# A table-driven cross-attention and maxout kernel: W's first three slices in nine pieces, and a new order for the head

## The chip, the core and the metric

The kernel runs on one core of a Trainium2 chip. The core has a matrix engine (PE, with its weight loads shown as PEld), a vector engine (DVE), a scalar engine (ACT), GpSimd (POOL) and a sync engine (SP) that here only issues transfers. The engines run side by side, each through its own list of instructions in order, and wait for each other through semaphores. Transfers of all queues run on the same 16 DMA engines. The metric is the time of one execution in microseconds (us), the median of three runs. It was 152.32 us before the change (152.24 to 152.41).

## What is computed

There are 8 batches of x with 8 heads, 512 tokens and 64 channels, and a state of 32 rows for each head. Two attentions run between them, and the result goes through a maxout layer with three weight matrices and an output layer:

```python
scores = scale * np.matmul(x, state.transpose(0, 1, 3, 2))   # a: softmax over the 32 states
xread = np.matmul(a, state)
scores2 = scale * np.matmul(state, x.transpose(0, 1, 3, 2))  # a2: softmax over the 512 tokens
sread = np.matmul(a2, x)
...
h = np.maximum(np.maximum(x @ w1, x @ w2), x @ w3)
return (h @ w_out).astype(np.float32)
```

In the last two lines `x` stands for the concatenated xread and sread, 544 tokens of each batch with 512 channels. w1, w2 and w3 are 512 by 768, w_out is 768 by 512.

## The kernel before

The kernel does not form xread. For each batch it multiplies the state into W first, which gives G = state x (w1, w2, w3), 256 rows by 3 x 768 columns. Then one matmul of the attention weights with G gives the first layer before the maximum. The 768 columns are cut into six slices of 128, numbered 0 to 5. "Slice m" of W is columns 128m to 128m+127 of all three matrices. A slice of G for a batch needs that slice of W from all three matrices.

What happens is written in tables of short operations (`FIRST`, `EACH`, `LAST`), and `perform` calls a function for each in turn. The text order sets, engine by engine, the order in which instructions stand; the order between engines comes from semaphores alone. `FIRST` holds the head: loading, batches 0 and 1, and the beginning of batch 2. `EACH` is one steady batch, and `LAST` the end. The operations that matter here, with the batch as first number:

- `lw m0 m1 i` (line 179) loads columns of slices m0 to m1-1 of matrix i, cast from float32 to bf16, on POOL's queue. A piece of one slice is 128 KB in bf16, with rows of 256 bytes; a piece of two slices is 256 KB, with rows of 512 bytes.
- `lxg b g`, `lx b` (lines 168, 163) load half or all of a batch of x on POOL's queue. `lst k` (line 152) loads the state of batches 2k and 2k+1, 128 KB of float32, on the queue of the engine named. `lwo` loads w_out.
- `xt`, `xtc` turn x on PE and copy it out of PSUM; `xtd` turns it by a DMA transpose from SP. `sc`, `ex`, `sum`, `wt` are scores, exponentials (ACT), sums (DVE) and attention weights; `at`, `atc` or `atd` turn these; `sr`, `srs` are sread.
- `g b m` (line 363) makes slice m of G for batch b, eight small matmuls, and `gc` copies it out of PSUM. `gr`, `grc` do the same for a run of columns. A `gc` or `grc` with `A` goes on ACT, with `D` on DVE, with `AD` half and half.
- `l1 b m` (line 416) is slice m of the first layer: six matmuls of 512 columns into three PSUM banks. `m0` (ACT), `ma`, `mb` (DVE) are its evictions, and free one bank each.
- `l2 b j`, `l2c` are the output layer for a quarter of the tokens and its copy; `so` stores.
- `stc`, `stt`, `stp` cast, turn and place a pair of states. `pad` (POOL) makes the padded copy of x for `sr`. `busy n` runs n matmuls of zeros that nothing reads.

PSUM is handed out by two strings: `BANKS` names one of four single banks for each use in turn, `PAIRS` one of two double banks. G's slices and a batch's scores take a pair, everything else a bank. A use waits for the copy that empties the bank.

A transfer on POOL's queue counts on one of eight semaphores in turn, so the ninth waits until the first has landed.

## Time and profile before

| | |
|---|---|
| runs | 152.32 us median of 3 (152.24 to 152.41) |
| profiled execution, span from first to last instruction | 151.4 us |
| median of the runs less that span | 0.9 us |
| granted TensorE clock | 1.000 of full speed |
| DVE, ACT, POOL busy | 118.9, 82.8, 57.0 us |
| moved by DMA | 22.29 MB, mean 147 GB/s |

The profile is of one execution. Times in it count from the span's start. In the lists of issues the last number is the time from the start of a transfer's issue to its landing; where a row holds several issues it is their median. Bytes of a transfer are counted as they are written, so a W piece of 128 KB was read as 256 KB.

### The profile page before, as it was taken

What the parts mean: (1) busy time and instruction counts of PE and PEld (TensorE: products, weight loads), DVE (VectorE), ACT (ScalarE), POOL (GpSimd) and SP (SyncE); (2) the same over time, 40 slices, a digit from 0 to 9 for tenths busy, and PEclk for the clock granted to TensorE, in tenths of its full rate; (3) what the DMA queues carried; (4) which work ended last, traced back from release to release, by engine and by line L of the source; (5) the groups of instructions that cost most, each with busy time, mean ns of one, the idle gap of its engine ahead of it and who ended that gap; (6) DMA issues with size and microseconds to landing.
All of it is one profiled execution on the core that took longest, in us unless ns stands there. A gap on an engine that the chain in (4) does not pass through costs nothing.

```text
span 151.4 us, 3635 instructions
## 1 busy us (share of the span) xinstructions
PE 146.4 (97%) x1431; PEld 73.8 (49%) x1431; DVE 118.9 (79%) x204; ACT 82.8 (55%) x143; POOL 57.0 (38%) x79
## 2 busy tenths in 40 slices
PE   6999799999999999999999999999999999999992
PEld 2566343335445443544354435443544446679771
DVE  6477698999977898879987988798879887675353
ACT  3368558976364665466646664666466653331220
POOL 6979650561528505540554046414331200001500
PEclk9999999999999999999999999999999999999999
DMA  3999999979737979999589749974503250300455
GB/s 115 211 189 195 207 198 195 151 149 139 139 74 167 230 59 265 129 223 132 155 124 230 144 130 140 232 122 141 218 0 78 68 226 4 122 18 17 175 180 196
DMA packets 39108, 22.29 MB, mean 147 GB/s; under 512 B 23072, under 2 KB 36896, under 8 KB 39088
## 3 DMA queue, kind: packets, MB, share of 16 engines
q0 software_dynamic: 15872, 13.96, 48.7%
q1 hardware_dynamic: 21776, 6.82, 23.4%
q10 hardware_dynamic: 1440, 1.25, 2.7%
q8 instruction: 12, 0.20, 0.5%
q14 instruction: 8, 0.07, 0.2%
HBM read 15.20 MB, written 8.91 MB: 159 GB/s over the span
## 4 chain that ended last, share of the span: by engine, by line
PE 86%; DMA 6%; POOL 4%; issue 1%; DVE 1%; POOLq 0%
PE pw L416 46%; PE po L447 25%; DMA w<-in_moe_w_dram 6%; PE pg L363 5%; PE po L462 4%; POOL w L179 2%; PE ps L262 2%; PE psr L327 2%; POOL x L168 1%; PE pgh L363 1%; PE pt L222 1%; DVE held L522 0%; PE idle L520 0%; PE idle L211 0%; DVE osb L466 0%
## 5 line engine op out<-in xcount | busy, mean ns | idle before, releaser
L416 PE MATMUL pw<-aT,G 128*128 128x512 bf16 x288 | 66.8, 379 | 0.0
L431 ACT CAST t<-pw 128x512 bf16<-128x512 f32 (+1 forms) x54 | 30.4, 564 | 28.9 <-PE pw L416 27.2
L416 PEld LDWEIGHTS <-G 128*128 128x128 bf16 x288 | 27.2, 98 | 33.2 <-issue 1.9
L436 DVE TENSOR_TENSOR t<-t,pw 128x512 bf16<-128x512 bf16 (+1 forms) x54 | 35.4, 655 | 9.5 <-ACT t L431 7.4
L447 PE MATMUL po<-wout,ht 128*128 128x512 bf16 x168 | 39.9, 379 | 0.0
L440 DVE TENSOR_TENSOR ht<-t,pw 128x512 bf16<-128x512 bf16 x48 | 32.9, 687 | 4.3
L447 PEld LDWEIGHTS <-ht 128*128 128x128 bf16 x168 | 15.3, 98 | 19.0 <-issue 1.7
L284 POOL TENSOR_TENSOR a<-e,rden 128x1024 bf16<-128x1024 bf16 (+1 forms) x9 | 14.5, 1620 | 24.1 <-ACT osb L454 11.1
L477 POOL DMA_DIRECT2D out_dram<-osb x13 | 7.4, 572 | 30.5 <-ACT t L431 27.5
L403 ACT CAST G<-pg 128x1024 bf16<-128x1024 f32 (+1 forms) x17 | 14.3, 875 | 1.3 <-PE pg L363 1.3
L311 POOL COPY xp<-x 128x1024 bf16<-128x1024 bf16 x12 | 12.3, 1062 | 5.5 <-DMA x<-in_x_dram 5.5
L454 DVE COPY osb<-po 128x512 f32<-128x512 f32 x16 | 10.9, 684 | 2.4 <-PE po L447 2.3
L276 DVE TENSOR_REDUCE seen<-e 128x32 f32<-128x1024 bf16 (+1 forms) x10 | 10.0, 999 | 3.6 <-ACT e L269 3.6
L403 DVE CAST G<-pg 128x1024 bf16<-128x1024 f32 (+1 forms) x13 | 12.2, 972 | 0.7 <-ACT G L403 0.7
L454 ACT COPY osb<-po 128x512 f32<-128x512 f32 x13 | 7.7, 593 | 8.9 <-PE po L447 8.9
L269 ACT ACTIVATE e<-ps 128x1024 bf16<-128x1024 f32 (+1 forms) x10 | 8.5, 854 | 6.6 <-PE ps L262 6.4
L363 PE MATMUL pg<-w,bd 64*32 64x512 bf16 (+1 forms) x288 | 10.8, 362 | 0.9 <-DMA w<-in_moe_w_dram 0.9
L211 PE MATMUL idle<-zero 128*128 128x512 bf16 x27 | 10.0, 477 | 1.3 <-DVE zero L187 1.3
L472 POOL DMA_DIRECT2D out_dram<-osb x4 | 2.2, 544 | 19.4 <-ACT osb L466 19.4
L381 ACT CAST G<-pg 128x768 bf16<-128x768 f32 x9 | 7.1, 801 | 3.3 <-PE pg L363 3.1
L416 PE MATMUL pw<-atp,w 128*128 128x256 bf16 x72 | 8.7, 272 | 0.0
L416 PEld LDWEIGHTS <-w 128*128 128x128 bf16 x72 | 6.9, 98 | 1.5
(70 smaller groups left out, 116.0 us busy)
## 6 DMA issues: line engine op xcount, KB each, us to landing
out_dram<-osb POOLq DMA_DIRECT2D x12, 512.0 KB, 3.5
x<-in_x_dram POOLq DMA_DIRECT2D x4, 512.0 KB, 7.3
x<-in_x_dram POOLq DMA_DIRECT2D x7, 256.0 KB, 5.5
w<-in_moe_w_dram POOLq DMA_DIRECT2D x4, 256.0 KB, 7.5
w<-in_moe_w_dram POOLq DMA_DIRECT2D x2, 384.0 KB, 7.9
wout<-in_moe_w_out_dram POOLq DMA_DIRECT2D x1, 768.0 KB, 11.6
out_dram<-osb SPq DMA_DIRECT2D x3, 256.0 KB, 2.4
osb<-in_x_dram SPq DMA_DIRECT2D x1, 512.0 KB, 4.0
```

Source lines behind the costliest of these rows:

```text
L211: nc.tensor.matmul(p, zero[:, 0:128], zero, start=True, stop=True)
L276: nc.vector.reduce_sum(out=den, in_=parity(e[b], g), axis=AX.X)
L284: times[c](out=parity(a[b], g).rearrange("p j g s n -> p j (g s) n"), in0=parity(e[b], g).rearrange("p j g s n -> p j (g s) n"), in1=rdens ...
L311: nc.gpsimd.tensor_copy(out=xp[b][:, :, :, g * (D + 1):g * (D + 1) + D], in_=v[:, g])
L363: nc.tensor.matmul(p(s, g), bd(b, 2 * s + g)[64 * g:64 * g + 64, g, :], f(w_sb[64 * g:64 * g + 64, s]), start=True, stop=True, tile_positi ...
L403: copier[c[g]](out=v[:, g:h], in_=p[:, g:h, 0:c1 - c0])
L416: nc.tensor.matmul(pw[i][:, 0:n], lhs(i, k), rhs(k), start=(k == 0), stop=(k == nk - 1))
L431: nc.scalar.copy(out=t0s[b, m][:, 0:n], in_=open_ps["l", b, m][0][:, 0:n])
L436: nc.vector.tensor_max(t1s[b, m][:, 0:n], t0s.pop((b, m))[:, 0:n], open_ps["l", b, m][1][:, 0:n])
L440: nc.vector.tensor_max(ht[b][:, m, :], t1s.pop((b, m))[:, 0:n], open_ps.pop(("l", b, m))[2][:, 0:n])
L447: nc.tensor.matmul(p, ht[b][:, m, j * 128:(j + 1) * 128], wout_sb[:, m, :], start=(m == 0), stop=(m == NM - 1))
L454: copier[c[i]](out=o[:, j, i * w:i * w + w], in_=p[:, i * w:i * w + w])
```

## The change

The tables `FIRST`, `EACH` and `LAST` become one table `PLAN`, written out for all batches. The code for the operations stays, with these differences: buffers of the rotating tiles are named in a table `PLACES`; the states' bf16 copies share two buffers where they had four; tiles are taken when they are first written, not when the matmuls ahead of them start; and the exponentials are written with the token quarters in the order 0, 2, 1, 3, which `sr` and the output layer then read in that order (`turned`). Operations for turning the scores by DMA (`sq`, `eq`, `etd`, `std`) are added to the list of operations, and the plan has none of them.

```diff
+    xt 1 0; ex 0 1; sum 0 0; busy 1; busy 1; xt 1 1; lw 0 1 2; xones 0; lw 0 1 1; lw 0 1 0; sum 0 1; xtc 1 1 D;
+    xtc 1 0 A; sc 1 0; lw 1 2 1; lw 1 2 2; lw 1 2 0; ex 1 0; lst 3 A; wt 0 1 D; lw 2 3 0; busy 1; busy 1;
...
-        nc.scalar.activation(out=parity(e[b], g), in_=open_ps.pop(("s", b, g)), func=AF.Exp, scale=scale)
+        new(e, b, [128, J, 2, HS, Ns], "e")
+        nc.scalar.activation(
+            out=parity(e[b], g).rearrange("p (c i) g s n -> p i c (g s n)", i=2),
+            in_=open_ps.pop(("s", b, g)).rearrange("p (i c) g s n -> p i c (g s n)", i=2),
+            func=AF.Exp, scale=scale)
...
+    def turned(j):
+        return j % 2 * 2 + j // 2
...
+    def buffer(shape, dtype, tag, key, name=None):
+        n = places[tag][str(key)] if places else str((B if key == "s" else key) % 2)
+        return work.tile(shape, dtype, tag=tag + n, bufs=1, name=name or tag)
...
-    perform(FIRST)
-    for b in range(2, B - 1):
-        perform(EACH, b)
-    perform(LAST)
+    perform(PLAN)
```

From batch 3's scores to the end the order on every engine is the one before (on PE, 1885 of some 2850 instructions of the main path). All that moves lies ahead of that: the head. 28 matmuls of zeros become 20. Three places follow.

**POOL, the loads of W.** Before, behind the last loads of batch 1's x. `x_87` is that x, `w` the weights, `a<-e,rden` the attention weights of batch 0 or 1.

```order
L168 DMA x_87<-in_x_dram 128x4x256 x2
L179 DMA w<-in_moe_w_dram 128x4x256 x2
L179 DMA w<-in_moe_w_dram 128x4x128
L179 DMA w<-in_moe_w_dram 128x4x256
L179 DMA w<-in_moe_w_dram 128x4x128 x2
L284 TENSOR_TENSOR a<-e,rden 128x4x128 x2
L198 MEMSET x_86 128x64
L179 DMA w<-in_moe_w_dram 128x4x128
L179 DMA w<-in_moe_w_dram 128x4x384 x2
L179 DMA w<-in_moe_w_dram 128x4x256
L284 TENSOR_TENSOR a<-e,rden 128x4x128
```

Now, at the same place:

```order
L206 DMA x_83<-in_x_dram 128x4x256 x2
L217 DMA w<-in_moe_w_dram 128x4x128
L236 MEMSET x_82 128x64
L217 DMA w<-in_moe_w_dram 128x4x128 x6
L349 TENSOR_TENSOR a<-e,rden 128x4x128
L217 DMA w<-in_moe_w_dram 128x4x128 x2
L217 DMA w<-in_moe_w_dram 128x4x384
L349 TENSOR_TENSOR a<-e,rden 128x4x128
L217 DMA w<-in_moe_w_dram 128x4x384
L217 DMA w<-in_moe_w_dram 128x4x128
L217 DMA w<-in_moe_w_dram 128x4x256
```

The first three slices came in six pieces, three of them of two slices; now they come in nine pieces of one slice, slice by slice. Slice 0 of all matrices stands behind three pieces of 384 KB in sum, where it stood behind three of 640 KB. Seven pieces stand ahead of the first product on POOL, where six stood; of three products on POOL one went to DVE. Of the pieces behind, those of slice 3 (two of 384 KB for slices 3 to 5 of two matrices, one of 128 KB for the third) now have the small one last.

**PE, the first layer's first slices.** Before, at the end of `l1 0 0` (`pw_427` is its third bank, `pg` a slice of G):

```order
L416 LDWEIGHTS G
L416 MATMUL pw_427<-aT,G 128x512 [waits DVE_49]
...
L363 LDWEIGHTS bd_82 [waits DMASW7_49,DMASW0_49]
L363 MATMUL pg<-w,bd_82 32x384 [waits Activation_49]
L363 LDWEIGHTS bd_82
```

Now, from the end of `l1 0 0` (`pw_424`) through `l1 0 1` (`pw_439` to `pw_441`):

```order
L477 MATMUL pw_424<-aT,G 128x512
L477 LDWEIGHTS G [waits Activation_49]
L477 MATMUL pw_439<-aT,G 128x512 [waits DVE_49]
...
L477 MATMUL pw_440<-aT,G 128x512 [waits Activation_49]
...
L477 MATMUL pw_441<-aT,G 128x512 [waits DVE_49]
...
L427 LDWEIGHTS bd_78 [waits DMASW3_49,DMASW2_49,DMASW1_49]
L427 MATMUL pg<-w,bd_78 32x384 [waits Activation_49]
```

Slice 2 of G for batches 0 and 1 stood right behind `l1 0 0`; now `l1 0 1`, six matmuls, comes ahead of it. Both turns of batch 1's weights (`at 1 0`, `at 1 1`) now come ahead of `l1 0 0`; one came behind slice 2 of G. Behind slice 2 there were four first-layer slices, now there are three, and then in both programs slice 3 of G for both batches.

**ACT, ahead of batch 2's exponentials.** Before, `e<-ps` being those exponentials, `t` an eviction `m0`, `bd` a placed state:

```order
L403 CAST G<-pg 128x2x512
L431 CAST t_691<-pw_645 128x512
L381 CAST G<-pg 128x6x128
L431 CAST t_748<-pw_680 128x512
L403 CAST G<-pg 128x512
L431 CAST t_757<-pw_715 128x512
L269 ACTIVATE e<-ps 128x1024
L228 COPY bd_84<-pt 64x16x32 x2
```

Now:

```order
L466 CAST G<-pg 128x2x512
L492 CAST t_632<-pw_621 128x512
L466 CAST G<-pg 128x2x512
L444 CAST G<-pg 128x6x128
L492 CAST t_670<-pw_655 128x512
L492 CAST t_702<-pw_692 128x512
L444 CAST G<-pg 128x6x128
L492 CAST t_726<-pw_708 128x512
L466 CAST G<-pg 128x2x512
L313 ACTIVATE e<-ps 128x2x2x256
L271 COPY bd_80<-pt 64x16x32 x2
```

Two whole copies of G that DVE did, one in full and one in half, are on ACT now, and `stp 1`, which the two shared, is on ACT alone. DVE has half of `gc 1 3` and the cast of a state in exchange.

Some more moves. `lst 3` and `lst 2` stood behind slice 3 of G (on SP and ACT) and are now issued on ACT with `lst 1`, just behind batch 1's exponentials. `stt 3` and `stt 2` stand together ahead of batch 2's scores, where one stood ahead and one behind. On POOL, `ones`, which waits for w_out, stands ahead of `pad 2`, and `lxg 3` behind it. On SP, `atd 2` stands ahead of `xtd 3`; the product `wt 2` that it turns went from POOL to DVE.

More of the change, by code (lines that the diff above doesn't have):

```diff
@@ new lines @@
+    ma 1 2; gc 0 4 A; l1 0 3; m0 0 3; stc 2 P; ones; gc 0 5 D; mb 1 2; gr 2 0 512; ma 0 3; gr 2 1792 2304;
+    l1 1 3; grc 2 0 512 A; m0 1 3; mb 0 3; grc 2 1792 2304 A; stc 3 D; ma 1 3; pad 2; g 1 4; mb 1 3; lxg 3 1;
+    l1 0 5; lxg 3 0; pad 3; gc 1 4 A; m0 0 5; ma 0 5; g 1 5; gr 2 1280 1792; l1 1 4; mb 0 5; m0 1 4; gc 1 5 A;
+    ma 1 4; mb 1 4; l1 0 4; gr 2 512 1024; m0 0 4; grc 2 1280 1792 A; ma 0 4; stt 3; stt 2; mb 0 4; sc 2 -;
+    l2 0 1; l2 0 0; ex 2 -; stp 2 A; sum 2 -; stp 3 A; l2 0 3; l2c 0 1 A; l2c 0 0 A; l1 1 5; wt 2 - D;
@@ L530 @@
-        "sc": (scores, 1), "ex": (exps, 1), "sum": (sums, 1), "wt": (weights, 1), "at": (a_turn, 1),
-        "atc": (a_turned, 1), "atd": (a_turn_dma, 1), "pad": (pad, 1), "sr": (sread, 1),
-        "srs": (sread_scale, 1), "srt": (sread_turn, 1), "ap": (sread_place, 1), "g": (g_slice, 1), "gc": (g_sliced, 1),
-        "gr": (g_run, 1), "grc": (g_ran, 1), "l1": (layer1, 1), "l1s": (layer1_states, 0),
-        "m0": (max_first, 1), "ma": (max_second, 1), "mb": (max_third, 1), "l2": (layer2, 1), "l2c": (layer2_out, 1),
@@ new lines @@
+        "stp": states_place, "std": states_turn_dma, "sts": states_place, "xt": x_turn, "xtc": x_turned, "xtd": x_turn_dma,
+        "sc": scores, "ex": exps, "sq": scores_turned, "eq": exps_turned, "etd": e_turn_dma, "sum": sums, "wt": weights, "at": a_turn,
+        "atc": a_turned, "atd": a_turn_dma, "pad": pad, "sr": sread,
+        "srs": sread_scale, "srt": sread_turn, "ap": sread_place, "g": g_slice, "gc": g_sliced,
+        "gr": g_run, "gq": lambda b, c0, c1: g_run(b, c0, c1, True), "gqc": g_ran, "grc": g_ran, "l1": layer1, "l1s": layer1_states,
```

248 lines of the change are left out of this document (148 added, 100 removed), and 3 rows, old and new, of the table BANKS.

## The prediction

> **What bounds the kernel now.** I read the page first, for the share of each engine.
>
> ```profile
> span 151.4 us, 3635 instructions
> PE 146.4 (97%) x1431; PEld 73.8 (49%) x1431; DVE 118.9 (79%) x204; ACT 82.8 (55%) x143; POOL 57.0 (38%) x79
> ```
>
> PE is busy all along, but zeros count there too, so the page cannot say when useful work becomes dense. The chain of waits can (start, length, what).
>
> ```profile
> 8.17 9.70 DMA w<-in_moe_w_dram
> ...
> 17.91 0.52 PE pg L363 x16
> ...
> 18.75 0.22 PE pat L295 x4
> 18.97 5.20 PE pw L416 x24
> 24.17 0.45 PE pg L363 x16
> 24.62 0.33 PE pt L222 x4
> 24.95 1.40 PE pw L416 x6
> ...
> 35.51 0.47 PE ps L262 x16
> ...
> 41.16 0.22 PE pt L222 x4
> ...
> 47.72 0.47 PE ps L262 x16
> ...
> 148.20 0.02 issue
> ```
>
> From 17.91 to 148.20 the chain is PE alone, and before that one load of W. So the time is the moment from which PE works without a gap, plus the work that is left. PE's own timeline shows how long it stood still there:
>
> ```profile
> 17.91 0.52 PE L363 MATMUL pg<-w,bd 64*32 64x384 bf16 x16 [0.86 <-DMA w<-in_moe_w_dram]
> ```
>
> The gap itself is 0.86 us, for slice 2 of G. Three points serve as milestones, since what lies between them can be counted in both programs: slice 3 of G (24.17), batch 2's scores (35.51) and batch 3's scores (47.72). From the last on, every engine has its old order, so I carry 47.72 to the end as it is.
>
> **When W lands.** Start and length of issues on POOL, and below them issues with the time to landing, each from a narrow window:
>
> ```profile
> 3.67 0.75 POOL L168 DMA_DIRECT2D x<-in_x_dram  x1
> 4.40 1.58 POOL L179 DMA_DIRECT2D w<-in_moe_w_dram  x2
> 5.97 1.50 POOL L179 DMA_DIRECT2D w<-in_moe_w_dram  x2
> 7.44 1.51 POOL L179 DMA_DIRECT2D w<-in_moe_w_dram  x2
> 13.66 1.50 POOL L179 DMA_DIRECT2D w<-in_moe_w_dram  x2
> ...
> x<-in_x_dram POOLq DMA_DIRECT2D x1, 256.0 KB, 6.0
> w<-in_moe_w_dram POOLq DMA_DIRECT2D x1, 256.0 KB, 6.7
> ...
> w<-in_moe_w_dram POOLq DMA_DIRECT2D x1, 256.0 KB, 7.3
> w<-in_moe_w_dram POOLq DMA_DIRECT2D x1, 128.0 KB, 7.2
> ...
> w<-in_moe_w_dram POOLq DMA_DIRECT2D x1, 256.0 KB, 7.8
> w<-in_moe_w_dram POOLq DMA_DIRECT2D x1, 128.0 KB, 7.8
> ...
> w<-in_moe_w_dram POOLq DMA_DIRECT2D x1, 384.0 KB, 8.6
> ```
>
> Added up: batch 1's x is there at 3.67 + 6.0 = 9.7. W's first pieces follow at 11.1, 12.4, 13.2 (5.97 + 7.2), 14.5 and 15.2 (7.44 + 7.8). The sixth, issued at 8.2, took the longest, 9.70, to 17.9 (the chain's first row). The last piece with slice 3 lands at 13.66 + 8.6 = 22.3. Landings follow each other in the order of issue, a queue that is always full; what counts is what stands ahead in it, not when a piece is issued.
>
> From these, a piece of two slices takes 1.33 us (11.1 to 12.4), one of one slice 0.74 (12.4 to 13.2 and 14.5 to 15.2). The change takes three pieces of two slices apart: 3 x (2 x 0.74 - 1.33) = 0.45 us more at most; half of it, if the rounding to 0.1 us of each landing goes the other way. I take 0.35. POOL issues in 0.75 a piece, as fast as pieces move, but seven are issued by 4.40 + 7 x 0.76 + 0.2 = 9.9, with x in the queue until 9.7, so it never runs dry there.
>
> The Trainium skill's "DMA: Bandwidth & Descriptors" (§ Specifications) asks for at least 512 bytes a transfer for the full rate and names a read-modify-write below; rows of one slice are 256 bytes as written. The rows above agree in sign only: 0.74 against half of 1.33.
>
> The state loads are the second cost. One was issued at 12.26, and the windows show what moved (last column GB/s):
>
> ```profile
> 12.26 0.35 ACTq L152 DMA_DIRECT2D stf<-in_state_dram  x1
> ...
> 13.00:14.00 1.00, 1.00 (x22) 0.47 (x20) 0.97 (x3) 0.89 (x2) 1.00 (x2) 1.00 1.62 186
> 14.00:15.00 1.00, 1.00 (x45) 0.72 (x44) 1.00 (x2) 0.66 (x2) 1.00 (x2) 1.00 1.72 207
> 15.00:16.00 1.00, 1.00 (x22) 0.45 (x20) 0.93 (x5) 0.95 (x3) 0.35 (x2) 1.00 1.61 228
> ```
>
> In the two us from 14 to 16, 435 KB moved where W alone makes 2 x 186 = 372. Of the 435, 131 are the state's 128 KB, so W got 304 and lost 68 KB, 0.37 us. Had a state load cost by its bytes, it would be 131/186 = 0.70. Two more loads now stand ahead of slice 3: 0.7 us by the first price, 1.4 by the second. I take 0.75, near the first, since it is this very load.
>
> Slice 3 then lands at 22.3 + 0.35 + 0.75 = 23.4, by the low ends 22.3 + 0.2 + 0.7 = 23.2, by the high ones 24.15. It may come up to half a us earlier: the sixth piece took 2.6 us behind the fifth, where one of its size takes 0.74, so something held it that no row names, and the same hold need not hit the same piece. I take 23.2.
>
> **When PE asks for it.** Slices 0 and 1 now come at 9.7 + 3 x 0.74 = 11.9 and 14.2, before the attention weights of batch 1 are ready, which `l1 0 0` now stands behind:
>
> ```profile
> 13.22 0.69 DVE L284 TENSOR_TENSOR a<-e,rden 128x512 bf16<-128x512 bf16 x1
> 13.83 0.95 DVE L381 CAST G<-pg 128x768 bf16<-128x768 f32 x1
> ...
> 15.41 0.25 DVE L278 RECIPROCAL rden<-seen 128x16 f32<-128x16 f32 x1
> ```
>
> Batch 1's second sums ended at 15.41 + 0.25 = 15.66. Ahead of them DVE had a copy of G of 0.95, now on ACT: 14.7. Then a short scaling of sread (an estimate of 0.4, less than the product's 0.69 for a quarter of its columns), the product (0.69) and four turns on PE (0.22 and a handoff): `l1 0 0` at 15.8, and it and `l1 0 1` end at 15.8 + 2 x 1.35 = 18.5 (a first-layer slice is 5.20/4 = 1.30 in a run, 1.40 alone). Slice 2 is due at 14.2 + 2.2 plus three state loads of 0.37, 17.5, and 18.7 if the old hold of 1.9 hits it in part. So PE begins it at 18.6, with 0.1 of waiting in place of 0.86. Then 0.45 for slice 2 and three first-layer slices of 1.30: PE asks for slice 3 at 22.95 and gets it at 23.2. That is 24.17 - 23.2 = **0.97 us won** at the first milestone. The gain is not what slice 0's earlier landing promises (1.3 us): PE gets ahead, and meets the loads again one slice later.
>
> **What is given back.** Between the first two milestones both programs have six first-layer slices and 80 small matmuls of G. Now there are four turns more (`stt 3`, 0.22, taken back between the second and third, row 41.16), and one more return from small matmuls to the first layer, 1.40 - 1.30 = 0.10. The larger question is ACT:
>
> ```profile
> 24.10:35.40 11.30, 11.30 (x127) 4.38 (x127) 10.71 (x17) 9.08 (x14) 4.88 (x8) 1.00 1.09 156
> ...
> L381 ACT CAST G<-pg 128x768 bf16<-128x768 f32 x5 | 3.9, 801 | 1.4 <-PE pg L363 1.3
> L431 ACT CAST t<-pw 128x512 bf16<-128x512 f32 x6 | 3.6, 594 | 0.1
> L403 ACT CAST G<-pg 128x1024 bf16<-128x1024 f32 x1 | 1.0, 1018 | 0.0
> L403 ACT CAST G<-pg 128x512 bf16<-128x512 f32 x1 | 0.6, 586 | 0.5 <-PE pg L363 0.5
> L228 ACT COPY bd<-pt 64x512 bf16<-64x512 bf16 x1 | 0.6, 582 | 0.0
> ```
>
> The rows add up to 9.7 us, 9.08 as they overlap, in 11.30 (the fifth number of the window's row; DVE 10.71). Now the stretch has six `t` (3.6), four casts of 768 (3.2), half a one (0.45), three of 1024 (3.05) and two `bd` (1.15): 11.45, or 10.7 overlapped. DVE sheds what ACT takes. So ACT does 10.7 of the 11.6 that PE needs, where DVE did 10.71 of 11.30 and PE lost nothing. A copy that ACT makes late holds a pair or a bank: `bd` of `stp 1` and two casts stand ahead of the pair that the run of batch 2's G asks for, and `grc 2 1280 1792`, which empties batch 2's pair for its scores, stands behind the last `m0`. I take 0.3 us for these, between nothing (as DVE's load cost before) and 1.8 (below).
>
> The other moves cost nothing while their covers hold. The first is x's transpose for batch 2, which shares the DMA engines with w_out (issued at 19.8; from the page):
>
> ```profile
> wout<-in_moe_w_out_dram POOLq DMA_DIRECT2D x1, 768.0 KB, 11.6
> ```
>
> w_out landed at 31.4, four us ahead of 35.51; 1.1 us more leaves room. `lxg 3` now waits on POOL for w_out and `pad 2`, and `xtd 3` on SP for `atd 2`; batch 3's scores, which they feed, stand 12 us behind batch 2's, and these are their cover. If it fails, what is missing there is added whole. The exponentials' new order has the same number of elements. Fewer zeros change nothing where PE waits anyway.
>
> **Sum.** Slice 3 at 23.2; batch 2's scores 11.34 + 0.22 + 0.10 + 0.30 = 11.96 later, 35.16; batch 3's 12.21 - 0.22 = 11.99 later, 47.15, against 47.72. That is 0.57 less: a span of 150.8 for 151.4, and with the 0.9 between span and median **151.75 us**. Its own range is 151.3 to 152.0.
>
> **Rivals.** (1) PE's side bounds, not the queue: no hold on slices 2 and 3. Then slice 3 starts at 18.5 + 0.45 + 3.9 = 22.85 and ACT costs nothing: 24.17 - 22.85 - 0.10 = 1.2 us won, 151.1. For it: the hold may hit another piece. Against: 0.45 and 0.7 us of longer transfers are in every row.
>
> (2) Nothing won: states at the price of their bytes and pieces at the high end, slice 3 at 24.15; all that was saved is given back, 152.3 to 152.5. For it: the queue is full all the time, and more stands in it.
>
> (3) Slower, by ACT between slice 3 and batch 2's scores. If ACT's rows don't overlap (11.45) and it waits for PE as it did (1.4 + 0.1 + 0.5 = 2.0), the stretch takes 13.45 in place of 11.66, 1.8 us more. With slice 3 at 23.2 that is 152.32 - 0.97 + 0.10 + 1.8 = 153.25. It decides from 1.0 us of ACT's lateness on. For it: 10.7 of 11.6 in a fixed order leaves 0.9; against: DVE's 95%.
>
> (4) The rate below 512 bytes. Were one-slice pieces at half the rate of two-slice ones, nine would take 9 x 1.33 = 12 us and not 6.7, slice 3 would land over 5 us later, and the time be near 156. Three such pieces stand in the rows at 0.74. [...]
>
> **Chances.** Forecast 0.40, (1) 0.14, (2) 0.18, (3) 0.27, (4) 0.01. A measurement of this kernel tells about 0.2% (0.3 us) from no change, so faster is below 152.0 and slower above 152.6. Faster: 0.40 + 0.14 = 0.54; the same 0.18; slower 0.28. The range of 150.9 to 153.2 runs from the far side of (1) to (3) and leaves the tail of (3) out.
>
> **What would show it.** Slice 0 of G near 12, `l1 0 1` ahead of slice 2, which starts near 18.6 with a wait of 0.1 to 0.3, and slice 3 near 23.2 behind a wait for W. The last piece of slice 3 lands 0.5 to 1.1 us later than 22.3. Batch 2's scores come 12.0 behind slice 3; over 12.7 speaks for (3), with PE waiting for ACT's copies of G or `bd`. A gap ahead of batch 2's or 3's scores with a DMA as its end would show a cover gone that I counted as safe. If slice 3 starts after 24.2, my prices of the loads are wrong.

## The result, and the profile after

| | before | changed |
|---|---|---|
| median of the runs | 152.37 us (6 runs, 152.20 to 154.95) | 163.74 us (6 runs, 160.66 to 165.54) |
| profiled execution, span | 151.4 us | 162.1 us |
| ratio | | 1.0589 [1.0513, 1.0665] |

The change makes the kernel slower. The ratio is taken from the two runs of the changed kernel with the higher granted clock; by the medians of all six it is 163.74 / 152.37 = 1.075, and each of the six lies more than 8 us above the median before.

The page of the changed kernel, its share of PE, the clock in 40 slices and the first group of instructions:

```profile
span 162.1 us, 3621 instructions
PE 147.3 (91%) x1423; PEld 73.8 (46%) x1423; DVE 116.9 (72%) x202; ACT 85.2 (53%) x146; POOL 56.2 (35%) x79
PEclk9999999999999998558999999999999999999999
L477 PE MATMUL pw<-aT,G 128*128 128x512 bf16 x288 | 67.9, 384 | 9.3 <-DMA aT<-a 9.3
```

PE works as long as before (147.3 us, 146.4 before) and stands still 10 us more. The first layer's matmuls waited 9.3 us in one piece for a transpose of attention weights, and around that place the clock falls to half.

PE's timeline of the changed kernel shows that this is not in the head (start, length, line, shape, and in brackets what it waited for):

```profile
12.11 0.52 PE L427 MATMUL pg<-w,bd 64*32 64x384 bf16 x16
...
15.19 2.75 PE L477 MATMUL pw<-aT,G 128*128 128x512 bf16 x12
...
18.88 0.64 PE L427 MATMUL pg<-w,bd 64*32 64x384 bf16 x16 [0.94 <-DMA w<-in_moe_w_dram]
...
23.45 0.52 PE L427 MATMUL pg<-w,bd 64*32 64x384 bf16 x16
...
35.12 0.63 PE L305 MATMUL ps<-bd,xT 128*128 128x64 bf16 x16
...
47.17 0.63 PE L305 MATMUL ps<-bd,xT 128*128 128x64 bf16 x16
```

Slice 0 of G comes at 12.11, slice 3 at 23.45 (24.10 in the same view of before), batch 2's scores at 35.12 (35.35), batch 3's at 47.17 (47.56). In this pair of profiles PE is 0.39 us ahead at the point from which every engine has its old order. The chain of waits of the changed kernel shows what came then (start, length, what):

```profile
60.46 10.12 DMA aT<-a
70.59 0.04 issue
70.63 2.72 PE pw L477 x6
73.35 0.75 PE ps L305 x16
74.10 1.30 PE po L514 x6
...
158.86 0.02 issue
```

The chain of before at the same work:

```profile
61.67 1.29 PE pw L416 x6
62.97 0.47 PE ps L262 x16
63.44 1.29 PE po L447 x6
```

`l1 3 0`, the first slice of batch 3's first layer, starts at 70.63 in place of 61.67, behind aT of batch 3, which took 10.1 us from its issue to its landing. Slice and scores behind the gap take 2.72 and 0.75 in place of 1.29 and 0.47. The sum is the whole loss of the profiled pair: 9.35 of gap and 1.71 of slow work, less the 0.39 that PE was ahead, make 10.67, and from 74.10 to 158.86 the distance to before stays at 10.66.

Why it took 10 us shows in the issues on SP and on POOL. SP's timeline of before (start, length, operation):

```profile
53.82 1.32 SPq L249 DMA_TRANSPOSE xT<-x  x1
55.24 2.20 SPq L346 DMA_TRANSPOSE ats<-sr  x1
57.55 1.24 SPq L302 DMA_TRANSPOSE aT<-a  x1
```

POOL's timeline of before, the issue of batch 4's x and that of the first store of batch 1:

```profile
45.12 0.90 POOL L163 DMA_DIRECT2D x<-in_x_dram  x1
...
58.57 0.61 POOL L477 DMA_DIRECT2D out_dram<-osb  x1 [5.56 <-ACT t L431]
```

SP's timeline of the changed kernel:

```profile
55.47 3.08 SPq L291 DMA_TRANSPOSE xT<-x  x1
58.61 1.75 SPq L410 DMA_TRANSPOSE ats<-sr  x1
60.46 1.33 SPq L366 DMA_TRANSPOSE aT<-a  x1
```

And POOL's, where batch 5's x and the second store follow the first:

```profile
45.59 0.89 POOL L201 DMA_DIRECT2D x<-in_x_dram  x1
...
58.18 0.61 POOL L548 DMA_DIRECT2D out_dram<-osb  x1 [5.57 <-ACT t L492]
58.79 0.92 POOL L201 DMA_DIRECT2D x<-in_x_dram  x1
59.68 0.56 POOL L548 DMA_DIRECT2D out_dram<-osb  x1
```

SP's list is the same in both: `xtd 4`, `srt 0`, `atd 3`. Before, `atd 3` goes out 1.02 us ahead of a burst of 1.5 MB on POOL's queue (two stores and batch 5's x). Now it goes out 2.28 us behind that burst. Counted from the issue of batch 4's x, the burst begins after 12.59 us (58.18 - 45.59) where it began after 13.45 (58.57 - 45.12). So of the 3.30 us between, 0.86 is x being issued nearer to the burst; 1.18 is x's own way (9.7 us to landing for 8.6), for which `xtd 4` waits; 1.76 is the issue of `xtd 4` itself, 3.08 for 1.32; the shorter `srt 0` gives 0.45 back. What that does to the transpose is in the DMA view of the changed kernel from 60.4 to 67.0, where q0 is POOL's queue and q1 SP's (packets, MB, and the time that the packets took as a share of 16 DMA engines' time; packets can overlap, so the shares can add up to more than 100%):

```profile
q0 software_dynamic: 1202, 1.15, 102.0%
q1 hardware_dynamic: 312, 0.07, 7.5%
```

### The profile page after: what moved, and what is told of

It is laid out like the page before. It is cut to its first block, busy times and chain, and to the rows that moved or that the text cites. A ratio compares the mean times of both kernels' runs of the same rounds, so it can differ in the third digit from the quotient of the medians.

```text
span 162.1 us, 3621 instructions
## 1 busy us (share of the span) xinstructions
PE 147.3 (91%) x1423; PEld 73.8 (46%) x1423; DVE 116.9 (72%) x202; ACT 85.2 (53%) x146; POOL 56.2 (35%) x79
## 4 chain that ended last, share of the span: by engine, by line
PE 55%; DMA 6%; DVE 1%; POOL 0%; issue 0%
PE pw L477 30%; PE po L514 15%; DMA aT<-a 6%; PE po L532 4%; PE pg L427 2%; PE ps L305 1%; PE psr L391 1%; PE pgh L427 1%; DVE held L593 0%; PE idle L591 0%; DVE osb L537 0%; POOL xp L372 0%; POOL xp L375 0%; PE pst L575 0%
## 5 line engine op out<-in xcount | busy, mean ns | idle before, releaser
L477 PE MATMUL pw<-aT,G 128*128 128x512 bf16 x288 | 67.9, 384 | 9.3 <-DMA aT<-a 9.3
L497 DVE TENSOR_TENSOR t<-t,pw 128x512 bf16<-128x512 bf16 (+1 forms) x54 | 35.4, 655 | 16.3 <-ACT t L492 10.1
L349 POOL TENSOR_TENSOR a<-e,rden 128x1024 bf16<-128x1024 bf16 (+1 forms) x7 | 11.7, 1675 | 29.8 <-ACT osb L526 21.4
L466 ACT CAST G<-pg 128x1024 bf16<-128x1024 f32 (+1 forms) x18 | 16.2, 931 | 0.8 <-PE pg L427 0.8
L466 DVE CAST G<-pg 128x1024 bf16<-128x1024 f32 (+1 forms) x10 | 9.7, 1004 | 7.1 <-ACT G L466 7.1
L375 POOL COPY xp<-x 128x1024 bf16<-128x1024 bf16 x12 | 12.9, 1113 | 3.8 <-DMA x<-in_x_dram 3.8
L526 ACT COPY osb<-po 128x512 f32<-128x512 f32 x15 | 8.7, 592 | 8.9 <-PE po L514 8.9
L526 DVE COPY osb<-po 128x512 f32<-128x512 f32 x14 | 9.6, 686 | 2.2 <-PE po L514 2.2
L217 POOL DMA_DIRECT2D w<-in_moe_w_dram x13 | 10.0, 783 | 0.0
L444 ACT CAST G<-pg 128x768 bf16<-128x768 f32 (+1 forms) x11 | 8.4, 780 | 2.5 <-PE pg L427 2.5
L249 PE MATMUL idle<-zero 128*128 128x512 bf16 x19 | 7.7, 501 | 1.4 <-DVE zero L225 1.3
```

Of the source, the lines that this page charges most:

```text
L217: nc.gpsimd.dma_start(out=w_sb[:, :, i, m0 * 128:m1 * 128], in_=(moe_w1, moe_w2, moe_w3)[i].rearrange("(kk p) f -> p kk f", p=128)[:, :, m ...
L349: times[c](out=parity(a[b], g).rearrange("p j g s n -> p j (g s) n"), in0=parity(e[b], g).rearrange("p j g s n -> p j (g s) n"), in1=rdens ...
L375: nc.gpsimd.tensor_copy(out=xp[b][:, :, :, g * (D + 1):g * (D + 1) + D], in_=v[:, g])
L466: copier[c[g]](out=v[:, g:h], in_=p[:, g:h, 0:c1 - c0])
L477: nc.tensor.matmul(pw[i][:, 0:n], lhs(i, k), rhs(k), start=(k == 0), stop=(k == nk - 1))
L497: nc.vector.tensor_max(t1s[b, m][:, 0:n], t0s.pop((b, m))[:, 0:n], open_ps["l", b, m][1][:, 0:n])
```

## Experiments

The theory is that collision: the head does roughly what was forecast, `atd 3` falls behind the burst, PE stands still, and its clock falls. The rivals are the head itself (nine pieces, state loads, ACT), and a transpose that is slow because it is late, not because of the burst. Each kernel below is the changed one, or the one before where that is said. Issue times are compared within one execution, since those of different executions can lie 1 us apart.

### The order on SP, and the stall made in the old kernel

`e1_aturn_first`:

```diff
-    ... m0 2 0; xtd 4; sc 3 -; ...  srt 0; ...  atd 3; ap 0 A;
+    ... m0 2 0; sc 3 -; ...  srt 0; ...  atd 3; xtd 4; ap 0 A;
```

> The changed kernel, but SP issues `atd 3` (the transpose of batch 3's attention weights) behind `srt 0` and ahead of `xtd 4`, not behind it. Theory: the whole loss is one collision. `xtd 4` waits for batch 4's x, which lands 1.65 us later than before; `atd 3`, queued behind it, is issued at 60.46 in place of 57.55, and its packets fall behind the 1.5 MB of stores and x that POOL issues from 58.18 on. With `atd 3` issued near 54.5 it lands by 58, PE does not stand still ahead of `l1 3 0`, the granted clock stays at 1.00, and the time is 151.6 to 152.2. Rival A (the head costs it: nine pieces, state loads, ACT): nothing of the head is touched, the time stays at 160 or above. Rival B (the burst hits whatever transpose comes next): `xtd 4` lands late and batch 4's scores wait, 155 or above.

Measured: 152.70 us (10 runs, 151.95 to 153.93), the kernel before 152.79 beside it, ratio 0.9984 [0.9954, 1.0014], clock 1.00. One line's place on SP takes back the whole loss, with the new head untouched; the rival that blames the head falls. The rest of the gain is missing: batch 4's x took 10.0 us, `xtd 4` 7.5, and batch 4's scores waited for it.

`e4_before_held`, the kernel before with tiny loads on SP (the edit is made in the pass of batch 2 alone, so `atd 1` is `atd 3` there):

```diff
     ... so -1 2 4 P; m0 0 4; ma 0 4; lx 3; mb 0 4;
+    hq 5;
     atd 1; ap -2 A; ...
+    def hold_queue(n):
+        for k in range(n):
+            nc.sync.dma_start(out=scratch[k], in_=state[0, 0, 0:1, 0:8])
```

> The kernel before, with five tiny loads (32 bytes each, not read by anything) on SP between `srt 0` and `atd 3`, each about 0.5 us of SP's issue: `atd 3` goes out near 60.2 in place of 57.55, all else as it was. Theory: the aT of batch 3 lands near 70, PE waits 8 to 10 us ahead of `l1 3 0`, the clock dips, 160 to 163. Rival A (the new head): 152.3. Rival C (a late issue costs its own lateness and no more): 2.7 us later is 60.35 + 2.7 = 63.0, against 60.9 when PE needs it, so 2 us at most, 154.5.

Measured: 160.6 us. The loads cost 0.3 us each, less than expected, so `atd 3` went out at 58.37, and the burst had begun at 58.13. From the chain of this run:

```profile
58.37 8.93 DMA aT<-a
67.30 0.04 issue
67.34 2.72 PE pw L417 x6
70.06 0.58 PE ps L263 x16
```

0.24 us behind the burst, and aT takes 8.9 us where it took 2.8 at 1.02 ahead of it. The old head has the same stall when this one issue is late. Counted from the issue of batch 4's x it is 1.26 us late (13.69 for 12.43); with 2.8 us to land, aT would have been there at 61.2, and PE, which ended its work at 61.24 and then waited 6.10, would have lost next to nothing. The tiny loads are not what slows aT: in `e15` below eight of them stand ahead of it, and it takes 2.8 us.

### Is it the burst, and which part of it?

`e7_pool_held` holds POOL ahead of the stores, with five copies that nothing reads:

```diff
-    l1 2 4; so 1 2 4 P; m0 2 4;
+    l1 2 4; hp 5; so 1 2 4 P; m0 2 4;
```

> The changed kernel with five copies of 128 x 512 floats on POOL (into a tile that nothing reads) ahead of `so 1 2 4`, 3 to 5 us: the burst of two stores and batch 5's x starts at 61 to 63 in place of 58.18, and `atd 3` is still issued at 60.46. Theory (the burst starves the transpose): with the burst behind it aT lands near 63.3, PE waits 2 us in place of 9.3, and the time is 153.5 to 156, the rest being what the later stores and x cost. Rival C (a transpose issued that late is slow by itself, or by what stands ahead of it on SP): aT lands 10 us after its issue, 160 or more.

Measured: 153.49 us. SP's issue and the first store on POOL:

```profile
57.99 1.24 SPq L367 DMA_TRANSPOSE aT<-a  x1
60.40 0.61 POOL L549 DMA_DIRECT2D out_dram<-osb  x1
```

aT landed 2.9 us after its issue, and PE waited 0.2 us for it. Without the copies the burst would have begun 12.59 us after the issue of batch 4's x, as in the changed kernel: 45.10 + 12.59 = 57.69, just ahead of `atd 3`. With the burst moved and nothing else, the stall is gone. (`atd 3` was earlier than expected, so the wait of 2 us did not come.) Lateness by itself is not the cause either: in `e18` below `atd 3` goes out at the same distance from x (12.94 us; here 12.89), but behind the burst, and aT takes 8.3 us.

`e8_x5_later` leaves the stores ahead and moves x:

```diff
-    ma 2 4; lx 5; mb 2 4; atd 3; ap 0 A; so 1 0 2 P; pad 4;
+    ma 2 4; mb 2 4; atd 3; ap 0 A; so 1 0 2 P; pad 4; lx 5;
```

> The changed kernel with batch 5's x (`lx 5`) behind `pad 4`, near 62 in place of 58.79; the two stores stay ahead of `atd 3`. It splits the burst. If the stores (1 MB) starve the transpose, aT still lands at 68 or later and the time is 158 or more. If it is the x load (512 KB in rows of 512 bytes), aT lands by 64.5 and the time is 153 to 156. If every byte ahead counts alike, about two thirds of the 9.3 us remain, 157 to 158.

Measured: 158.77 us; in its chain:

```profile
58.94 5.24 DMA aT<-a
64.17 0.04 issue
64.21 2.72 PE pw L477 x6
```

aT landed at 64.2, as expected if x were what starves it: 1 MB of stores makes 5.2 of 2.8 us, and the other 3 to 8 us of the runs with the whole burst need x in it. The time is above that guess's 156, since a gap of 3.5 us already lowers the clock (below). The packets in the traces tell the two parts of the burst apart, since x's are of 512 bytes and the stores' of some 4 KB. In `e8`, while the stores alone moved (59.5 to 61.5), SP's queue got 159 packets through, 80 a us. In the changed kernel, while x alone moved on POOL's queue (61.5 to 65.5, 874 packets), SP's queue got 44, 11 a us. Both starve it, x more. Two runs were to show x alone, the stores behind `pad 4`: `e11_stores_later`, with two copies on POOL to hold x at its place, and `e15_x5_alone`, with eight tiny loads on SP as well.

```diff
-    l1 2 4; so 1 2 4 P; m0 2 4; ma 2 4; lx 5; mb 2 4; atd 3; ap 0 A; so 1 0 2 P; pad 4;
+    l1 2 4; hp 2; m0 2 4; ma 2 4; lx 5; mb 2 4; hq 8; atd 3; ap 0 A; pad 4; hp 5; so 1 2 4 P; so 1 0 2 P;
```

(That is `e15`; `e11` has neither `hq 8` nor `hp 5`.)

> The other half of the burst: the two stores of batch 1 go behind `pad 4` (issued after 60.5), and batch 5's x stays ahead of `atd 3`, issued at about 58.5 behind two copies of POOL that hold it there (they write a tile that nothing reads). With the stores alone ahead, aT took 5.2 us to land; with both, 10 to 13. If the bytes add up, x alone should give 2.8 + (10.1 - 5.2) = 7.7 us. If only stores delay a transpose: 3 to 4 us. If x alone is what starves it: 9 us or more. The time is near 152.5 plus what lies over 4 us in that landing, plus 1.5 to 3 us of lower clock if PE stands still over 3 us.

> The changed kernel with the two stores of batch 1 late (behind `pad 4` and five copies on POOL, after 64), batch 5's x at 59.4 as the only large transfer, and `atd 3` held to about 60.4 by eight tiny loads, so that it comes behind x and ahead of the stores. With the two stores ahead and x behind, aT took 5.2 us to land, with all three 10 to 13. Additive bytes: 7.7 us. Stores alone to blame: 3 to 4 us. x alone to blame: 9 us or more.

Measured: 153.48 and 159.61 us, and neither has what it was made for. In `e11` batch 4's x happened to land early, `atd 3` went out at 57.58, ahead of x (59.44), and aT took 3.2 us. In `e15` the tiny loads were through only at 61.9, `atd 3` went out at 62.56, 4.8 us behind x and when x was nearly done (it landed at 63.7), and aT took 2.8 us; its 159.61 us are the lateness itself, with PE waiting 5.2 us and a lower clock. How long an aT right behind x alone takes stays unmeasured; the nearest to it is `e2` in the next part.

### Why SP is late

`e3_before_x4_late` (the kernel before) and `e2_x4_early`, `e6_x4_behind_stores` (the changed kernel) move the load of batch 4's x:

```diff
 e3
-    so 0 0 2 P; lx 4; so 0 2 4 P; stp 3 A;
+    so 0 0 2 P; so 0 2 4 P; lx 4; stp 3 A;
 e2
-    lxg 3 0; pad 3; ...  so 0 2 4 P; lx 4; atd 2;
+    lxg 3 0; pad 3; lx 4; ...  so 0 2 4 P; atd 2;
 e6
-    so 0 2 4 P; lx 4; atd 2; ...  xtd 4; sc 3 -; ...  so 0 0 2 P;
+    so 0 2 4 P; atd 2; ...  sc 3 -; ...  so 0 0 2 P; lx 4; xtd 4;
```

> The kernel before, with `lx 4` behind both stores of batch 0 and not between them: x is issued about 0.6 us later, 45.7, and queues behind another 512 KB. Theory: x lands at 54.5 to 56 in place of 53.68, `atd 3` is issued after 59.3, and the kernel before gets the same stall: 158 to 163 if `atd 3` comes after the burst at 58.6, in part if it comes just with it. Rival A (the stall needs the new head): 152.3 as before, by 0.3.

> The changed kernel, but batch 4's x (`lx 4`) is issued behind `pad 3`, ahead of the first store, at about 41.7 in place of 45.59; SP's order is untouched. Theory: x lands before 53, `xtd 4` no longer waits for it, `atd 3` is issued by 58 ahead of the burst, no stall, 151.6 to 152.2. Rival A (the head): 160 or above. Rival B (SP is late for another reason, the buffer of `xtd 4` or the slow issue of 3.08 us): `atd 3` still after 60, 160 or above.

> The changed kernel with `lx 4` behind both stores of batch 0 and nothing else: SP still issues `xtd 4`, `srt 0`, `atd 3` in that order. Theory (the loss hangs on whether `atd 3` goes out ahead of the burst at 58.2): if x lands by 54, `atd 3` goes out by 57.9, and there is no stall, 151.2 to 152.2; if it lands at 55 or later as it did, `atd 3` comes after 60 and the stall is there whole, 160 or more. Nothing between the two. Rival A (the head costs it): 160 or more in both cases.

Measured: 152.21, 157.59 (4 runs, 155.29 to 166.02) and 165.34 us. The first expectation failed: behind both stores x landed not later but earlier, 7.2 us from its issue. The second failed in a way that tells more. With x out at 41.63, `xtd 3`, issued at 41.14, met it, and the chain shows the same collision one batch earlier:

```profile
41.14 8.67 DMA xT<-x
49.81 0.05 issue
49.86 0.93 PE ps L305 x16
```

The stores came at 45.06, 3.9 us behind `xtd 3`, which otherwise lands in 4.3 (the changed kernel). From 45.5 to 48.0 POOL's queue moved 746 packets of some 512 bytes, which are x's, and SP's queue 25; so most of the other 4.4 us passed while x moved. The reverse shows too: from x's issue at 41.63 to 45.0, with `xtd 3` ahead of it, SP's queue moved 2259 packets and POOL's one.

The third is between its two cases: x landed at 54.1, but `xtd 4` took 3.18 us to issue, `atd 3` went out at 58.78, 1.49 behind the burst at 57.29, and aT took 13.0 us.

`e9_x3_old_place` undoes the part of the change that delays `xtd 3`:

```diff
-    ... pad 2; g 1 4; mb 1 3; lxg 3 1; l1 0 5; lxg 3 0; pad 3; ...
+    ... lxg 3 1; lxg 3 0; pad 2; g 1 4; mb 1 3; l1 0 5; pad 3; ...
-    so 0 2 4 P; lx 4; atd 2; ...  grc 3 0 512 A; xtd 3;
+    so 0 2 4 P; lx 4; xtd 3; atd 2; ...  grc 3 0 512 A;
```

> The changed kernel with one part of the change undone: batch 3's x is loaded ahead of `pad 2` again (`lxg 3 1; lxg 3 0` right behind `ones` on POOL), and `xtd 3` stands ahead of `atd 2` on SP again, as in the kernel before. `xtd 4`, `srt 0`, `atd 3` keep their order, `lx 4` its place. Theory (the chain of lateness begins here): x of batch 3 lands at about 37.7 in place of 38.96, `xtd 3` goes out at 37.8 in place of 41.13, its packets are gone from the rings about 1 us earlier, so batch 4's x, issued at 45 to 45.6, lands at 53 to 53.7 in place of 54 to 55.3, `atd 3` goes out ahead of the burst at 58, and the time is 151.5 to 152.5 with a granted clock of 1.00. Rival: x of batch 4 is late for another reason (order of the stores, a ring that lags): it lands after 54 all the same, `atd 3` goes out after 58.3, and the time is 158 or more. Rival A (nine pieces, state loads, ACT): 160 or more.

Measured: five of ten runs at 151.69 to 152.27, five at 162.78 to 165.88, nothing between. The five without the stall have a ratio to the kernel before of 0.9958 [0.9928, 0.9987]. In the profiled run, one with the stall, `xtd 3` was early (36.38) and batch 4's x landed late all the same, 9.4 us after its issue. So the chain of lateness that I supposed, from batch 3's x to batch 4's, did not decide in that run.

`e13_changed_again` is the changed kernel unaltered, `e16_srt_early` takes `srt 0` out of the stretch, `e18_x3_and_srt` has the edits of `e9` and `e16` together:

```diff
-    ... m0 2 0; xtd 4; sc 3 -; ...  srt 0; ma 2 3; ...
+    ... m0 2 0; srt 0; xtd 4; sc 3 -; ...  ma 2 3; ...
```

> The changed kernel, unaltered, as the measure for the three others. If the stall is a matter of a margin that the change made too small (the burst starts 12.59 us after the issue of batch 4's x, where it was 13.45, and what must fit between took 10.8 to 14.9 us in the profiles so far), some runs should be free of it and come out near 152.0, most at 160 to 166, and nothing between 154 and 158. If it is tied to the change in every run: all at 160 to 166.

> The changed kernel with `srt 0` ahead of `xtd 4` on SP, where SP waits anyway; `xtd 4` and `atd 3` keep their order. It takes 1.2 to 2.2 us out of what must fit between x's landing and the burst and touches nothing else. By the sum, the changed kernel's profile (x at 55.33) would come to 58.65 and still be 0.5 us behind the burst, the three others with its head and a late `atd 3` (58.78, 58.94, 58.88, bursts at 57.29, 57.59, 57.62) to 57.4 to 57.6, on the edge or ahead. Theory: more than half of the runs near 152.0, the others above 156. Rival (the stall does not hang on that sum): all runs as the changed kernel's.

> The changed kernel with batch 3's x and `xtd 3` at their old places (half of the runs with that alone were free of the stall, at 151.7 to 152.3) and `srt 0` ahead of `xtd 4` (nine of ten free with that alone). Theory: both widen the same margin, so nearly all runs are free of it, and the median is 151.9 to 152.4 where the kernel before shows 152.4 to 152.9, a ratio of 0.995 to 0.999. Rival: the head is worth nothing, ratio 1.000. Rival: the stall is still there in some runs, so the margin is not what these two moves change.

Measured: the changed kernel 165.40 (4 of 4 runs with the stall, 163.65 to 166.06; 10 of 10 with the first six). With `srt 0` early, nine of ten runs at 151.85 to 153.35 and one at 162.36. With both, against expectation and on another chip, one run of six at 151.63 and the others at 155.36 to 165.62. In its profiled run x took 9.7 us and `xtd 4` 3.04 to issue, so `atd 3` went out at 57.77, 0.35 behind the burst. The two edits don't add up; in the profiles with the first of them (`e9`, `e12`, `e18`) x still took 8.5 to 9.7. Ten of the profiled runs, all with the whole burst and with `atd 3` behind `xtd 4`, each with all times from the issue of batch 4's x:

| run | x lands | `atd 3` issued | burst begins | `atd 3` | aT to landing |
|---|---|---|---|---|---|
| before | 8.6 | 12.43 | 13.45 | 1.02 ahead | 2.8 |
| `e3` (old head) | 7.2 | 10.80 | 12.89 | 2.09 ahead | 3.4 |
| `e4` (old head) | 8.1 | 13.69 | 13.45 | 0.24 behind | 8.9 |
| changed | 9.7 | 14.87 | 12.59 | 2.28 behind | 10.1 |
| `e13` | 9.5 | 14.01 | 12.58 | 1.43 behind | 11.8 |
| `e6` | 8.8 | 13.50 | 12.01 | 1.49 behind | 13.0 |
| `e9` | 9.4 | 13.85 | 12.59 | 1.26 behind | 11.3 |
| `e18` | 9.7 | 12.94 | 12.59 | 0.35 behind | 8.3 |
| `e16` | 8.5 | 10.80 | 12.59 | 1.79 ahead | 4.5 |
| `e10` | 7.3 | 11.22 | 12.59 | 1.37 ahead | 3.2 |

In this table every run ahead of the burst has its aT within 4.5 us, every run behind it after 8.3 or more; `e17` and `e14` (below, old head, 0.90 and 1.97 behind) have 11.1 and 10.3. Far ahead is no promise by itself: in `e1`, 5.5 us ahead of the burst but with batch 4's x still landing, aT took 6.7 us, which PE did not notice. The burst column is set by the order: 13.45 in the kernel before, 12.59 in the changed one, and 12.89 and 12.01 where x stands behind both stores (`e3`, `e6`). How early PE is does not move it: among the profiles with 12.59 batch 3's scores come anywhere from 46.15 to 47.17. The `atd 3` column varies from run to run by up to 4 us. So the changed kernel has the stall nearly always, not always: `e10` is the same program up to that place and escaped. Of 81 runs of the kernel before, one took 158.52 at a lower clock; there is no profile of it.

### The clock

`e10_zeros_in_gap` puts 40 matmuls of zeros ahead of `l1 3 0`; `e14_before_held_zeros` and `e17_more_zeros` put 28 and 40 there in the kernel before, with the stall forced by eight tiny loads:

```diff
-    l1 3 0; m0 3 0;
+    fill 40; l1 3 0; m0 3 0;
```

> The changed kernel with 40 matmuls of zeros (512 columns, read by nobody) on PE just ahead of `l1 3 0`, where PE stands still for 9 us: they take 8.6 us of that wait and change nothing of what it waits for. Theory: the wait for aT stays (`l1 3 0` begins about 10 us after `atd 3`'s issue), but the granted clock does not fall, `l1 3 0` takes 1.3 us and not 2.72, batch 4's scores 0.47 and not 0.75, and the time is 1.4 to 1.8 us below the changed kernel's of the same length of wait, 161.5 to 162.5 if the wait is as long as in its profile. Rival: the slow slices behind the gap come from the DMA traffic, not the clock: still 2.7 us.

> The kernel before, with `atd 3` held behind the burst by eight tiny loads on SP (five were enough for a stall of 6 us), and 28 matmuls of zeros ahead of `l1 3 0`, 6.0 us that PE would wait anyway. Theory: aT still takes 9 us or more to land, but with PE at work the granted clock stays at 1.00, `l1 3 0` takes 1.3 to 1.5 us and not 2.72, and the loss is the gap alone: 1.5 us or more below what a gap of that length costs without zeros (start of `l1 3 0` less 61.0, plus 152.5, gives the time to 0.5 us). Rival: the slices behind the gap are slow for another reason (2.7 us again, clock at 0.5).

> The kernel before with eight tiny loads on SP ahead of `atd 3`, as in the run with 28 zeros, and 40 matmuls of zeros (8.6 us) ahead of `l1 3 0`. There, PE ended its zeros at 66.7, `l1 3 0` began at 69.92 and took 2.47 us, batch 4's scores 0.85, and the output slice behind them 1.56 (1.32, 0.47 and 1.29 undisturbed): 2.0 us and a little for the clock. Theory: with the gap filled to within 1.5 us the clock stays at 1.00, these take their undisturbed times, and the time is (start of `l1 3 0` less 60.7) + 152.5 within 0.5 us. Rival (not the clock): 2.4 to 2.7 us for `l1 3 0` again.

Measured: 161.81, 163.45 and 161.83 us. The first had no gap to fill, so its zeros were 8.6 us of plain work; it tells nothing of the clock. In the second the zeros ended 3.2 us before aT landed (at 69.87), and in the third they reached to it. Windows of 4 us of the second (length, busy time of PE, PEld, DVE, ACT, POOL with counts, granted clock, DMA share, GB/s):

```profile
66.00:70.00 4.00, 0.79 (x5) 0.18 (x3) 0.00 (x0) 0.00 (x0) 0.00 (x0) 1.00 1.03 134
70.00:74.00 4.00, 4.00 (x26) 2.00 (x27) 1.38 (x2) 1.25 (x2) 0.00 (x0) 0.57 0.60 113
```

The same windows of the third:

```profile
66.00:70.00 4.00, 3.88 (x18) 1.55 (x16) 0.00 (x0) 0.00 (x0) 0.00 (x0) 1.00 0.77 180
70.00:74.00 4.00, 3.88 (x60) 1.85 (x64) 2.17 (x3) 1.96 (x4) 0.00 (x0) 1.00 0.74 139
```

3.2 us of rest are enough to halve the clock (in `e2`, 2.5 us); with PE at work to the end it stays at 1.00. The chain of the third has undisturbed lengths:

```profile
59.03 11.05 DMA aT<-a
70.08 0.05 issue
70.12 1.47 PE pw L424 x6
71.59 0.47 PE ps L270 x16
```

There `l1 3 0` begins 8.45 us later than in the profile of before (70.12 - 61.67) and takes 0.18 longer; the span is 8.6 us longer (160.0 for 151.4), so the gap is the whole loss. What the clock adds behind a gap, by the length of the same three pieces of work (3.05 us undisturbed), is 1.5 us in `e4`, 1.7 in the changed kernel, 1.8 in the second of these runs and 2.9 in `e8` and `e13`, whether the gap was short (3.5 us in `e8`) or long (10.1 in `e13`). The Trainium skill's "TensorE: Matmul & The Clock Gate" (§ What's actually happening) has the array at half clock after an idle window of about 3.4 us and at full clock again after about 3.4 us of work. The traces agree in size and not in a fixed figure: the granted clock fell 2.1 us (`e4`) to 5.4 us (`e13`) after PE's last matmul, and came back 2.8 us (`e4`) to 5.6 us (`e8`) after work began.

### What the head is worth

`e5_both_moved` has the edit of `e1` with x behind both stores, `e12_x3_and_aturn` that of `e1` with that of `e9`:

```diff
 e5
-    so 0 2 4 P; lx 4; atd 2; ...  so 0 0 2 P;
+    so 0 2 4 P; atd 2; ...  so 0 0 2 P; lx 4;
 e5, e12
-    ... xtd 4; sc 3 -; ...  atd 3; ap 0 A;
+    ... sc 3 -; ...  atd 3; xtd 4; ap 0 A;
```

> The changed kernel with two moves: `atd 3` ahead of `xtd 4` on SP (as in the run with that move alone), and `lx 4` behind both stores of batch 0 on POOL (in the kernel before, that place let batch 4's x land 7.2 us after its issue, where it took 10.0 in the run with the first move alone). There, x landed at 54.8, `xtd 4` was issued so late that the burst from 57.4 on hit it (7.5 us to landing), and batch 4's scores waited 1.1 to 1.7 us. Theory: with x at 52 to 53 `xtd 4` lands by 58.5, nothing waits, and the head's gain of 0.4 to 1.0 us is kept: 151.2 to 152.0 where the kernel before shows 152.4 to 152.8. Rival: x lands as late as it did there, whatever its place, 152.7. Rival: the head gains nothing, so that a kernel free of the collision equals the one before, 152.5.

> Both repairs: x of batch 3 and `xtd 3` at their old places, and `atd 3` ahead of `xtd 4`. The new head is otherwise whole (nine pieces, three state loads early, l1 0 1 ahead of slice 2). Theory: no transpose meets a burst, the head's gain is kept: 0.3 to 0.6 us below the kernel before, 151.9 to 152.5 where that shows 152.4 to 152.9. Rival: the head is worth nothing once the collision is gone, a ratio of 1.000. Rival: another transpose is late, 153 or more.

Measured: 152.39 us (12 runs, 152.01 to 154.39; before 152.85, ratio 0.9982 [0.9957, 1.0007]) and 152.35 (12 runs, 151.88 to 153.60; before 152.59, ratio 0.9987 [0.9963, 1.0010]). In both PE goes through batch 4's scores without a wait. None of the 34 runs with `atd 3` ahead of `xtd 4` has the stall: all lie from 151.88 to 154.39 us, at a clock of 0.997 or more. The three ratios, 0.9982 to 0.9987, each with 1 inside its interval, put the head at 0.2 to 0.3 us, which isn't told from nothing, and the nine runs of `e16` without the stall say the same (0.9982 [0.9948, 1.0015]). Only the five runs of `e9` tell a gain (0.6 us), and these are five picked out of ten by how they came out. In the profiles, batch 3's scores come at 46.55 to 47.56 with the old head (five) and at 46.03 to 47.73 with the new one (fourteen; `e2`, where the scores themselves wait, left out), 0.4 us apart in the mean and each spread over 1 us or more.

## Why the prediction was wrong

The step that failed is the last of the first part: "From the last on, every engine has its old order, so I carry 47.72 to the end as it is." The order is the old one; the distances are not. In that stretch the prediction put the wait for batch 3's aT at nothing, and it came to 9.35 us, with 1.71 of slow work behind it. Three things run through the stretch: POOL's issue of batch 4's x, SP's list, and PE, which releases the burst. The burst comes 11.01 us behind batch 3's scores in both profiles (58.57 - 47.56, 58.18 - 47.17). x goes out 1.58 us ahead of these scores (47.17 - 45.59) where it went out 2.44 ahead (47.56 - 45.12): 0.86 of a margin of 1.02 that stands in the rows of before (57.55 against 58.57); the later batches have 2.8 and more there (70.96 against 73.78). The rest went by the longer way of x and the longer issue of `xtd 4`. The 0.86 comes from the order of the tables, not from PE's being ahead, since every profile with the new head and its own place of `lx 4` has it. Before, `lx 4` stood behind the first store, `so 0 0 2`; now it stands behind `so 0 2 4`. This move stands neither in the list of moves nor in the prediction. That it is what costs the 0.86 is read from the rows; no run restored that order alone.

Point by point:

- **When W lands, and when PE asks.** Slice 0 at 12.11 (near 12), `l1 0 1` ahead of slice 2, slice 2 at 18.88 (18.6). Its last piece of W landed at 18.7, as in my case with part of the old hold; but `l1 0 0` had begun at 15.19, not 15.8 (my own terms add up to 16.0), so PE was ready at 17.94 and waited 0.94, not 0.1 to 0.3. The last piece of slice 3 landed at 23.3, as forecast, and slice 3 came at 23.45 (23.2) and waited for PE, not for W. So 0.65 us were won there (24.10 - 23.45), not 0.97. The term was right in kind and too large by a third. The wait of 0.86 that it set out to save was in part that one execution's: of the five profiles with the old head, only that of before shows PE waiting for W ahead of slice 2, and slice 3 comes at 23.09 to 23.67 in the other four.
- **What is given back.** Batch 2's scores came 11.67 behind slice 3 (35.12 - 23.45), 0.42 more than before (11.25), where I had 0.62 more. Of that, 0.32 are the turns and the return that I had counted; ACT gave back 0.1 at most. Rival (3) did not happen, and my 0.30 for it was too much.
- **Batch 3's scores.** 0.39 ahead of before, against my 0.57. The two errors cancel in part, so the nearness of these two numbers is partly luck.
- **The covers.** I looked at `xtd 3` and found 12 us of cover to batch 3's scores. That held. What I did not ask is what stands behind it: x of batch 4, `xtd 4`, `srt 0`, `atd 3`, each late for the next, against a burst of stores that comes at its old distance behind batch 3's scores. My own last paragraph named the sign, a gap with a DMA as its end, and placed it a batch too early.
- **Rivals.** Without the collision 0.2 to 0.3 us are left, between rival (2)'s nothing and the forecast's 0.57; the 1.2 us of rival (1) show in no set of runs. (4) fell: slices of 256-byte rows did not double, slice 3 was not late. The rival that happened, a transfer turned from covered to starved in the part that does not change, was not among them, so the range had no place for 11 us.

What stays open: why batch 4's x takes 8.5 to 10.0 us in most runs with the new head and 7.2 to 8.6 with the old, and why `xtd 4` issues in 1.32 us in the old and in 1.7 to 3.3 in the new. The edit that was to bring x earlier (`e9`) did not. Two things in the traces narrow it. A load has sixteen landings, and in all profiles but two (`e2`, `e6`) fifteen of x's are there 7.1 to 7.7 us after its issue, with either head; the sixteenth comes up to 2.6 us behind them (in the changed kernel at 9.7, the fifteenth at 7.35). So it is one share of x in sixteen that is late. And the long issue is not the new head's own: in the profile of before the same instruction for batch 5 takes 2.95 us (at 66.63).

## What to carry to other kernels

Where a prediction says that a stretch keeps its order, look up the margins between the engines there, above all between a small transfer that PE needs and a large one that PE's own progress releases: a load that moves to another place upstream can use up such a margin, though nothing in the stretch itself has changed. A transpose that PE waits for belongs ahead of one that is not due yet and waits for a load, and here that one place was worth 11 us. A kernel can sit on such an edge, so that the same program takes 152 or 164 us; look at all of the runs, not only at the median.

## What the hardware showed

- **One queue starves another.** From 60.4 to 67.0 POOL's queue had 102.0% of the engines' time and SP's 7.5%, and a transpose of 2.8 us took 10.1. The effect has an edge: 1.02 us ahead of the burst nothing, 0.24 behind it 6 us more. In that run (`e4`) SP's queue moved 1024 packets from 59.5 to 63.0 and only 32 in the 4.3 us from there to aT's landing; an aT has 1056 (`e15`, 63.5 to 65.3), so its last 3% held PE up. The Trainium skill's "DMA: Bandwidth & Descriptors" (§ Queues, rings and completion order) has each engine take the queues that have work in turn, a packet at a time. By that the transpose should have lost a part of its rate; the rows show it nearly stopped (44 of its packets to 874 while x moved), and no run shows why.
- **The burst is slow itself.** In those 6.6 us it moved 1.15 MB, 174 GB/s, at full engines. In the profile of before, with no transpose under way, x alone (61.5 to 65.5) moved 0.45 MB at 108.6%, 114 GB/s; two stores alone moved 0.78 MB in 2 us at 96.5% (`e8`, 59.5 to 61.5). x is a load that casts, written in rows of 512 bytes.
- **A short rest costs twice.** 2.5 to 3.2 us without work halve the clock (`e2`, `e14`), and what the slow work behind a rest adds (1.5 to 2.9 us) can come near the rest itself.
